# Moving a ninth MLP unit into the attention, and the first weight conversions into its first steps

## The chip, the cores and the metric

The kernel runs on one core of one Trainium2 chip. The metric is device time in microseconds of one execution, the median over several runs. TensorE ran at its upper clock level (2.4 GHz; mean granted clock 0.998) in the profiled execution.

## The reference

Attention with a soft cap over 4 batches, 12 heads, 448 tokens and head dimension 64, then a three-way maximum MLP over 1792 tokens of width 768, all float32.

```
scores = cap * tanh(scale * q @ k.T / cap)          # scale = 1 / sqrt(64)
attn   = exp(scores - max) ; attn = attn / (sum(attn) + 1e-9)
x      = (attn @ v)  with heads joined               # 1792 x 768
h      = max(max(x @ w1, x @ w2), x @ w3)            # 1792 x 768
out    = h @ w_out                                   # 1792 x 768
```

## The kernel before

**Attention.** A step t (0 to 11) handles one batch and a group of four heads; batch t // 3, group t % 3. Keys are cut into seven tiles j of 64. For each tile TensorE makes the scores (`scores`, L120: eight float32 matmul instructions on 64x64 quadrants) into one of two PSUM buffers `qk` in turn; ScalarE takes tanh out of PSUM (`tanh`, L129) and exp in SBUF (`expo`, L132); TensorE multiplies the exponentials with v (`values`, L135) into the PSUM tile `av`; VectorE adds the exponentials up (`add`, L143). At the start of the next step TensorE sums over the keys with a matrix of ones (`sums`, L147) into the PSUM tile `sm`, in two halves for the steps in BY_PE, whose seventh exponential TensorE adds instead of VectorE. VectorE makes the reciprocals with two transposes (`recip`, L157), multiplies (`normalize`, L166), and splits the result into a high and a low float32r part in `xx` (`split_x`, L170). The maximum is not subtracted: with a small cap the exponentials can't overflow, and a branch takes the general form otherwise.

**Order.** All orders are written out by hand. Function `step` (L268) lists the instructions of all engines in one sequence; each engine takes its own from it in order, and waits where an operand or buffer isn't ready. `scores(t+1, 0..2)` and `tanh(t+1, 0)` already stand at the end of step t, and `scores(t+1, 2)`, the last of them, needs the buffer that `tanh(t+1, 0)` reads.

**MLP units.** A unit (n, b) multiplies one weight tile n (128 outputs; n = 3f + w, matrix w of output tile f, n from 18 on for w_out) with the tokens of one block b: `products` (L227), 18 float32r matmuls, three for each of six input chunks. Block 0 has 256 tokens, blocks 1 to 3 have 512. Block 0 needs batch 0 (steps 0 to 2), block 1 steps 0 to 5, block 2 steps 0 to 8, block 3 all. `empty` (L238) copies the result with ScalarE for w = 0, and takes the maximum into it with VectorE for w = 1, 2. A table FILL puts eight units into the middle of steps 4 to 11, ahead of `scores(t, 5)`; they use half of `sm`. The unit (2,2) is done right behind the attention (FILLED), then units (0,3) and (1,3), whose chunks 4 and 5 come last because they need step 11. All other units follow in order of n and b (`mlp`, L379).

**Weights.** A weight tile arrives as 64-bit floats (768 KB), and six instructions (`conv`, L200, steps 0 to 5) make the float32r high and low parts. Tables CONV, SCALED and LOADS say in which attention steps these instructions and the DMAs stand; in step 0 the first tile's conversions stand between the adds. Tiles use two raw buffers `wd`, two work buffers `cw` and three result buffers `wh`, `wl`.

**Start and end.** `first` holds q of step 0 and the cap in one array of 897 columns; it, k, v and the first weight tile are loaded on ScalarE's DMA queue, later ones on SP's. The very last bank, (23, 3), is copied in two halves of 256 tokens, one by VectorE and one by ScalarE, each with its own store.

Of the kernel before, what the change touches and what calls it, by code (L numbers as in the profile page):

```python
# [29 lines left out]
CAP_LO = 1e-6  # L30
WARM = 7

FILL = {4 + i: (i % 3, i // 3) for i in range(8)}
FILLED = [(2, 2)]
BY_PE = (0, 1, 2, 3, 11)
CONV = {0: [(0, 4), (0, 5)], 1: [(1, 0), (1, 1)], 2: [(1, 2), (1, 3)], 3: [(1, 4), (1, 5), (2, 0)],
        4: [(2, 1), (2, 2)], 5: [(2, 3), (2, 4), (2, 5)], 9: [(3, 1)], 10: [(3, 2), (3, 3)]}
SCALED = {9: 3}
LOADS = {0: 1, 1: 2, 6: 3, 11: 4}


@with_exitstack
def attn_max_mlp_kernel(ctx: ExitStack, tc: tile.TileContext, first, q, k, v, wts, out):
# [113 lines left out]
    def recip(t, eps):  # L157
        x, r = x_t[t % 2], r_t[t % 2]
        nc.vector.transpose(out=x, in_=sm[:, :, 0:S])
        nc.vector.tensor_scalar_add(r, flat(x).rearrange("p (a b) -> p a b", b=32)[:, :, 0], eps)  # L160
        nc.vector.reciprocal(r, r)
        nc.vector.transpose(  # L162
            out=flat(x).rearrange("p (a b) -> p a b", b=32), in_=r.unsqueeze(2).to_broadcast([128, 2 * QB, 32])
        )
# [73 lines left out]
    def empty(n, b, ps):  # L238
        f, w = divmod(n, 3)
        at = slice(*BLOCKS[b])  # L240
        ps = ps[:, 0:at.stop - at.start]
        if n < 3 * KC:
            m = m_t[f][:, at]
            if w == 0:
                nc.scalar.copy(out=m, in_=ps)
            else:
                tt(nc.vector, m, m, ps, ALU.max)
            return
        dst = out[n - 3 * KC][:, at]
        o = o_t[outs[0] % len(o_t)][:, 0:at.stop - at.start]  # L250
        outs[0] += 1
        if (n, b) == (NU - 1, NB - 1):
            one, two = slice(0, 256), slice(256, 512)
            nc.vector.tensor_copy(out=o[:, one], in_=ps[:, one])
            nc.sync.dma_start(out=dst[:, one], in_=o[:, one])
            nc.scalar.copy(out=o[:, two], in_=ps[:, two])
            nc.scalar.dma_start(out=dst[:, two], in_=o[:, two])
        else:
            nc.scalar.copy(out=o, in_=ps)
            nc.sync.dma_start(out=dst, in_=o)  # L260
# [7 lines left out]
    def step(t, eps):  # L268
        last = t - 1
        if 0 < t < NG - 1:  # L270
            load_qk(t + 1)
        if t:
            sums(last, last in BY_PE)
            recip(last, eps)
        if t == NG:
            for j in range(4, NJ):
                values(last, j)
            normalize(last)
            split_x(last)
            return  # L280
        fill = FILL.get(t)
        tanh(t, 1)
        expo(t, 0)
        scores(t, 3)
        if t:
            values(last, 4)
            values(last, 5)
        tanh(t, 2)
        expo(t, 1)
        add(t, 1)  # L290
        scores(t, 4)
        if t:
            values(last, 6)
            normalize(last)
        tanh(t, 3)
        expo(t, 2)
        add(t, 2)
        if t:
            split_x(last)
        if 0 < t < NG - 1:  # L300
            load_v(t + 1)
        if t in LOADS:
            conv_load(LOADS[t])
        if fill:
            products(*fill, sm[:, 0, :], range(KC))
        tanh(t, 4)
        expo(t, 3)
        if fill:
            expo(t, 4)
            empty(*fill, sm[:, 0, :])  # L310
        if t in SCALED:
            conv(SCALED[t], 0, True)
        add(t, 3)
        if t == 0:
            conv(0, 0)
            conv(0, 1)
        scores(t, 5)
        if not fill:
            tanh(t, 5)
            expo(t, 4)  # L320
            scores(t, 6)
            values(t, 0)
        else:
            values(t, 0)
            tanh(t, 5)
            scores(t, 6)
        add(t, 4)
        if t == 0:
            conv(0, 2)
        values(t, 1)  # L330
        if t + 1 < NG:
            scores(t + 1, 0)
        values(t, 2)
        if fill:
            expo(t, 5)
            tanh(t, 6)
        else:
            tanh(t, 6)
            expo(t, 5)
        add(t, 5)  # L340
        if t == 0:
            conv(0, 3)
        if t + 1 < NG:
            scores(t + 1, 1)
        expo(t, 6)
        if t not in BY_PE:
            add(t, 6)
        for n, i in CONV.get(t, []):
            conv(n, i)
        values(t, 3)  # L350
        if t + 1 < NG:
            tanh(t + 1, 0)
            scores(t + 1, 2)

    def general_attention():
        for t in range(NG):
# [22 lines left out]
    def mlp(done, convs):  # L379
        g = 0  # L380

        def bank():
            nonlocal g
            g += 1
            return banks[(g - 1) % 8]

        def whole(n, b):
            ps = bank()
            products(n, b, ps, range(KC))
            empty(n, b, ps)  # L390
            done.add((n, b))

        fast = bool(done)
        if fast:
            for n, b in FILLED:
                whole(n, b)
            held = []
            for n in range(2):
                held.append(bank())
                products(n, NB - 1, held[n], range(KC - 2))  # L400
            for n in range(2):
                products(n, NB - 1, held[n], range(KC - 2, KC))
                empty(n, NB - 1, held[n])
                done.add((n, NB - 1))
                if n == 0:
                    for i in (4, 5):
                        conv(3, i, True)
        for n in range(NU):
            if 3 <= n and n + 2 < NU:
                conv_load(n + 2)  # L410
            for b in range(NB):
                if (n, b) not in done:
                    whole(n, b)
                if n >= 3 and n + 2 < NU:
                    for i in convs[b]:
                        conv(n + 2, i, True)
                elif n == 2 and b == NB - 1:
                    for i in range(6):
                        conv(4, i, True)
                elif not fast and n == 0 and b == NB - 1:  # L420
                    for i in (4, 5):
                        conv(3, i, True)
                if n == 3 * KC - 1:
                    for f in range(KC):
                        split_h(b, f)
# [2 lines left out]

    with tc.manual_schedule():
        nc.sync.dma_start(out=k_t[0][:, 0:2].rearrange("p a b c -> p (a b c)"), in_=k[0, :, 0:256])  # L430
        nc.scalar.dma_start(out=q_0[:, 0:2 * S + 1], in_=first)
        nc.scalar.dma_start(out=k_t[0][:, 2:].rearrange("p a b c -> p (a b c)"), in_=k[0, :, 256:])
        load_v(0, nc.scalar)
        conv_load(0, nc.scalar)
        nc.vector.memset(wz.bitcast(F32), 0.0)
        for _ in range(WARM):
            nc.tensor.matmul(sm[:, 0, 0:S], wz[:, 0:128], wz, start=True, stop=True)
        nc.gpsimd.memset(ones, 1.0)
        nc.gpsimd.memset(eps_g, 1e-9)
        nc.scalar.activation(out=acap, in_=cap_t, func=AF.Abs)  # L440
        nc.vector.tensor_scalar(out=fl, in0=acap, scalar1=CAP_HI, scalar2=None, op0=ALU.is_le)
        nc.vector.scalar_tensor_tensor(
            out=fl_i, in0=acap, scalar=CAP_LO, in1=fl, op0=ALU.is_ge, op1=ALU.mult
        )
        nc.vector.reciprocal(sc_t, acap)
        nc.vector.tensor_scalar_mul(sc_t, sc_t, 1.0 / float(D) ** 0.5)
        nc.scalar.activation(out=eps_f, in_=acap, func=AF.Exp, scale=-1.0)
        nc.vector.tensor_scalar_mul(eps_f, eps_f, 1e-9)
        scores(0, 0)
        scores(0, 1)  # L450
        tanh(0, 0)
        scores(0, 2)
        flag = nc.values_load(fl_i[0:1, 0:1], min_val=0, max_val=1)
        with tc.If(flag > 0) as br:
            load_qk(1)
            load_v(1)
            for t in range(NG + 1):
                step(t, eps_f)
            mlp({*FILL.values()}, convs)
        outs[0] = 0  # L460
        with br.Else():
            general_attention()
            conv_load(1)
            for n in range(3):
                for i in range(6):
                    conv(n, i)
                conv_load(n + 2)
            for i in range(4):
                conv(3, i)
            mlp(set(), convs)  # L470
# [49 lines left out]
```

## Time and profile before

| what | value |
|---|---|
| median of 3 runs | 509.86 us (509.38 to 510.35) |
| profiled execution, its own time | 509.67 us |
| span of its trace | 507.9 us |
| busy VectorE, ScalarE | 259.8 us (51%), 229.3 us (45%) |
| attention (steps 0 to 11 with the last normalization) | up to about 183.5 us |

The span is the time from the first to the last instruction; the time of an execution is 1.8 us longer. Engine names in the rows: PE is TensorE, PEld its weight loads, DVE is VectorE, ACT is ScalarE, SPq and ACTq are DMA issues of these queues. An instruction's line is that of the helper that records it, so L102 is every VectorE operation on two tensors, and the tile names tell which one it is.

### The profile page before, as it was taken

The numbers are of one execution on the slowest core, as the hardware profiler recorded it, in microseconds if no ns is written. First come the engines' busy times: TensorE is split into PE (matmuls) and PEld (weight loads), VectorE is DVE, ScalarE is ACT, GpSimd is POOL, SyncE is SP. The second block draws the span as 40 slices with busy tenths as digits, with TensorE's granted clock in tenths as the row PEclk, the third lists the DMA queues.
The fourth block names the chain that finished last, engine by engine and source line by source line (L and its number), as shares of the span: only waits on it lengthen the run. The fifth ranks groups of instructions, "written<-read, shape, count | busy, mean of one in ns | idle before, by whom it ended". The sixth has DMA issues, their size and how long they took to land.

```text
span 507.9 us, 7474 instructions
## 1 busy us (share of the span) xinstructions
PE 494.1 (97%) x3215; PEld 350.7 (69%) x3215; DVE 259.8 (51%) x332; ACT 229.3 (45%) x285; POOL 0.4 (0%) x6
## 2 busy tenths in 40 slices
PE   6899999999999999999999999999999999999996
PEld 2333344444455568888888888888888888888884
DVE  1889999987778963334323413332341577212000
ACT  6999999979888711410121121021122355221210
POOL 0000000000000000000000000000000000000000
PEclk9999999999999999999999999999999999999999
DMA  7343333413232100301301111120121101333111
GB/s 280 135 172 111 110 110 110 167 42 110 74 111 98 63 1 0 125 12 52 124 1 62 63 62 63 41 85 0 63 72 54 63 1 52 136 114 136 69 56 68
DMA packets 12423, 41.44 MB, mean 82 GB/s; under 512 B 1376, under 2 KB 2528, under 8 KB 12384
## 3 DMA queue, kind: packets, MB, share of 16 engines
q1 hardware_dynamic: 11664, 38.74, 22.0%
q10 hardware_dynamic: 720, 2.16, 1.1%
q8 instruction: 27, 0.44, 0.3%
q14 instruction: 12, 0.10, 0.1%
HBM read 35.39 MB, written 5.51 MB: 81 GB/s over the span
## 4 chain that ended last, share of the span: by engine, by line
PE 88%; ACT 6%; DVE 3%; issue 1%; DMA 1%; ACTq 0%; DVEq 0%
PE qk L232 9%; PE qk L233 9%; PE qk L234 9%; PE qk L124 9%; PE av L138 8%; PE sm L232 8%; PE sm L234 8%; PE sm L233 8%; PE av L234 6%; PE av L232 6%; PE av L233 6%; ACT e_all L130 3%; ACT e_all L133 3%; PE sm L152 3%; DVE s_t L102 1%
## 5 line engine op out<-in xcount | busy, mean ns | idle before, releaser
L232 PE MATMUL qk<-xx,wh 128*128 128x512 f32 (+1 forms) x264 | 89.6, 339 | 0.0
L233 PE MATMUL qk<-xx,wh 128*128 128x512 f32 (+1 forms) x264 | 89.6, 339 | 0.0
L234 PE MATMUL qk<-xx,wl 128*128 128x512 f32 (+1 forms) x264 | 89.3, 338 | 0.0
L130 ACT ACTIVATE e_all<-qk,sc_t 128x896 f32<-128x896 f32 x84 | 83.3, 1006 | 10.9 <-PE qk L124 10.4
L133 ACT ACTIVATE e_all<-e_all,acap 128x896 f32<-128x896 f32 x84 | 86.5, 1046 | 0.5
L124 PE MATMUL qk<-q,k_t 64*64 64x448 f32 x672 | 78.7, 543 | 7.0 <-ACT e_all L130 6.2
L138 PE MATMUL av<-e_all,v_t 64*64 64x448 f32 x672 | 74.9, 536 | 0.0
L221 ACT CAST wh<-cw 128x768 fp32r<-128x768 f32 x21 | 17.5, 835 | 116.2 <-DVE cw L217 116.2
L232 PE MATMUL sm<-xx,wh 128*128 128x512 f32 (+1 forms) x180 | 69.0, 383 | 0.0
L234 PE MATMUL sm<-xx,wl 128*128 128x512 f32 (+1 forms) x180 | 68.2, 379 | 0.0
L233 PE MATMUL sm<-xx,wh 128*128 128x512 f32 (+1 forms) x180 | 68.1, 378 | 0.0
L102 DVE TENSOR_TENSOR s_t<-s_t,e_all 128x896 f32<-128x896 f32 x55 | 59.8, 1088 | 10.3 <-ACT e_all L133 8.3
L124 PEld LDWEIGHTS qk<-q,k_t 64*64 64x64 f32 x672 | 23.2, 132 | 47.1 <-ACT e_all L130 21.5
L232 PEld LDWEIGHTS qk<-xx,wh 128*128 128x128 f32 x264 | 50.1, 190 | 6.3 <-issue 0.7
L234 PEld LDWEIGHTS qk<-xx,wl 128*128 128x128 f32 x264 | 50.0, 189 | 5.6
L233 PEld LDWEIGHTS qk<-xx,wh 128*128 128x128 f32 x264 | 50.1, 190 | 5.4
L138 PEld LDWEIGHTS av<-e_all,v_t 64*64 64x64 f32 x672 | 25.5, 133 | 37.6 <-issue 36.1
L232 PE MATMUL av<-xx,wh 128*128 128x512 f32 x132 | 51.3, 389 | 0.0
L233 PE MATMUL av<-xx,wh 128*128 128x512 f32 x132 | 51.3, 389 | 0.0
L234 PE MATMUL av<-xx,wl 128*128 128x512 f32 x132 | 51.3, 389 | 0.0
L102 DVE TENSOR_TENSOR wl<-cw,wh 128x768 fp32r<-128x768 f32 x24 | 23.0, 956 | 42.9 <-ACT wh L221 35.4
L232 PEld LDWEIGHTS sm<-xx,wh 128*128 128x128 f32 x180 | 33.8, 188 | 11.7 <-DVE x_t L162 4.9
(66 smaller groups left out, 414.8 us busy)
## 6 DMA issues: line engine op xcount, KB each, us to landing
wd<-in_wts_dram SPq DMA_DIRECT2D x23, 768.0 KB, 4.2
k_t<-in_k_dram SPq DMA_DIRECT2D x11, 448.0 KB, 3.4
q<-in_q_dram SPq DMA_DIRECT2D x11, 448.0 KB, 4.5
v_t<-in_v_dram SPq DMA_DIRECT2D x11, 448.0 KB, 3.3
out_dram<-q SPq DMA_DIRECT2D x6, 256.0 KB, 2.0
out_dram<-s_t SPq DMA_DIRECT2D x6, 256.0 KB, 2.0
out_dram<-x_t SPq DMA_DIRECT2D x5, 256.0 KB, 2.0
wd<-in_wts_dram ACTq DMA_DIRECT2D x1, 768.0 KB, 6.9
```

The costliest lines, as they stand in the source:

```text
L102: eng.tensor_tensor(out=out, in0=in0, in1=in1, op=op)
L124: nc.tensor.matmul(ps[rows(s), R, 0:S], k_t[t % 2][rows(R), j, s, :], q_t[t % 2][rows(R), s, :], start=True, stop=True, skip_group_check=True,
L130: nc.scalar.activation(out=e_of(t, j), in_=slot(t, j)[:, :, 0:S], func=AF.Tanh, scale=sc_t)
L133: nc.scalar.activation(out=e_of(t, j), in_=e_of(t, j), func=AF.Exp, scale=acap)
L138: nc.tensor.matmul(av[rows(R), s, 0:S], v_t[t % 2][rows(s), j, R, :], e_of(t, j)[rows(s), R, :], start=(j == 0), stop=(j == NJ - 1), skip_ ...
L152: nc.tensor.matmul(sm[rows(R), s, 0:S], ones[rows(s), :], part[rows(s), R, :], start=(i == 0), stop=(i == len(parts) - 1), skip_group_chec ...
L221: nc.scalar.copy(out=h, in_=d)
L232: nc.tensor.matmul(ps, w_h, a_h, start=(kc == 0), stop=False)
L233: nc.tensor.matmul(ps, w_h, a_l, start=False, stop=False)
L234: nc.tensor.matmul(ps, w_l, a_h, start=False, stop=(kc == KC - 1))
```

## The change

Unit (2,2) moves into the attention. Units (0,0), (0,1) and (0,2) now stand at the end of steps 3, 6 and 9 (table LATE), behind `scores(t+1, 2)`, and are emptied in the next step ahead of its sums; the other six stand in the middle of steps 4, 5, 7, 8, 10 and 11. The sums in steps 4, 7 and 10 move behind `scores(t, 3)` and the emptying. Weight tiles 0 and 1 are both converted in step 0, tile 2 in steps 1 to 3 (it was steps 3 to 5), and the first two instructions of tile 3 move from step 9 to step 8. The loads of weight tile 0 and 1 are both issued at the start, tile 0 ahead of v. `first` gets 960 columns in DRAM, of which 897 are loaded. The last weight tile takes its blocks in the order 1, 2, 3, 0, so that the last bank has 256 tokens, copied in halves of 128.

```
-FILL = {4 + i: (i % 3, i // 3) for i in range(8)}
-FILLED = [(2, 2)]
+LATE = {3: (0, 0), 6: (0, 1), 9: (0, 2)}
+FILL = {4: (1, 0), 5: (2, 0), 7: (1, 1), 8: (2, 1), 10: (1, 2), 11: (2, 2)}
-CONV = {0: [(0, 4), (0, 5)], 1: [(1, 0), (1, 1)], 2: [(1, 2), (1, 3)], 3: [(1, 4), (1, 5), (2, 0)],
-        4: [(2, 1), (2, 2)], 5: [(2, 3), (2, 4), (2, 5)], 9: [(3, 1)], 10: [(3, 2), (3, 3)]}
-SCALED = {9: 3}
-LOADS = {0: 1, 1: 2, 6: 3, 11: 4}
+CONV = {1: [(2, 0), (2, 1)], 2: [(2, 2), (2, 3)], 3: [(2, 4), (2, 5)], 8: [(3, 1)], 10: [(3, 2), (3, 3)]}
+SCALED = {8: 3}
+LOADS = {1: 2, 6: 3, 11: 4}
+FIRST = {0: [(0, 0), (0, 1), (0, 2), (0, 3)], 1: [(0, 4), (0, 5)], 2: [(1, 0)], 3: [(1, 1)], 4: [(1, 2)],
+         5: [(1, 3), (1, 4), (1, 5)]}
...
-        if (n, b) == (NU - 1, NB - 1):
-            one, two = slice(0, 256), slice(256, 512)
+        if (n, b) == (NU - 1, 0):
+            one, two = slice(0, 128), slice(128, 256)
...
+        late, fill = LATE.get(last), FILL.get(t)
...
+        if t and not late:
+            normalizing()                     # sums(last), recip(last)
...
+        if t == 0:
+            convs(FIRST[0])                   # FIRST[j] stands behind add(0, j) for j = 1 to 5
         tanh(t, 1)
         expo(t, 0)
         scores(t, 3)
+        if late:
+            tanh(t, 2)
+            empty(*late, sm[:, 0, :])
+            normalizing()
         if t:
             values(last, 4)
             values(last, 5)
-        tanh(t, 2)
+        if not late:
+            tanh(t, 2)
         expo(t, 1)
         add(t, 1)
...
         if t + 1 < NG:
             tanh(t + 1, 0)
             scores(t + 1, 2)
+        if t in LATE:
+            products(*LATE[t], sm[:, 0, :], range(KC))
...
-            for n, b in FILLED:
-                whole(n, b)
...
-            for b in range(NB):
+            for b in range(NB) if n < NU - 1 else (1, 2, 3, 0):
...
-        nc.scalar.dma_start(out=q_0[:, 0:2 * S + 1], in_=first)
+        nc.scalar.dma_start(out=q_0[:, 0:2 * S + 1], in_=first[:, 0:2 * S + 1])
         nc.scalar.dma_start(out=k_t[0][:, 2:].rearrange("p a b c -> p (a b c)"), in_=k[0, :, 256:])
+        conv_load(0, nc.scalar)
         load_v(0, nc.scalar)
-        conv_load(0, nc.scalar)
+        conv_load(1, nc.scalar)
...
-            [qq[0, 0].reshape(128, 2 * S), _np.broadcast_to(_np.asarray(inputs["cap"]).reshape(1, 1), (128, 1))], axis=1
+            [qq[0, 0].reshape(128, 2 * S), _np.broadcast_to(_np.asarray(inputs["cap"]).reshape(1, 1), (128, 64))], axis=1
```

## Rows read from the trace of the kernel before

**Rows 1.** The page, busy time, share of the span and instructions by engine.
```profile
PE 494.1 (97%) x3215; PEld 350.7 (69%) x3215; DVE 259.8 (51%) x332; ACT 229.3 (45%) x285; POOL 0.4 (0%) x6
```

**Rows 2.** Windows: length, busy us (instructions) by engine, clock, DMA share, GB/s.
```profile
46.16:59.19 13.03, 12.25 (x129) 4.71 (x129) 12.42 (x15) 12.90 (x15) 0.00 (x0) 1.00 0.34 108
150.37:166.15 15.78, 15.78 (x143) 7.70 (x139) 12.31 (x14) 13.72 (x17) 0.00 (x0) 1.00 0.22 80
```

**Rows 3.** Timeline, TensorE, steps 3 to 7: start, us, engine, line, operation, [idle before].
```profile
59.19 0.98 PE L124 MATMUL qk<-q,k_t 64*64 64x448 f32 x8 [0.78 <-ACT e_all L130]
...
81.54 0.98 PE L124 MATMUL qk<-q,k_t 64*64 64x448 f32 x8
...
87.60 0.97 PE L124 MATMUL qk<-q,k_t 64*64 64x448 f32 x8
...
101.43 0.98 PE L124 MATMUL qk<-q,k_t 64*64 64x448 f32 x8
102.95 0.98 PE L152 MATMUL sm<-s_t,ones 64*64 64x448 f32 x8 [0.54 <-DVE s_t L102]
...
107.62 0.50 PE L232 MATMUL sm<-xx,wh 128*128 128x512 f32 x1
...
111.94 0.98 PE L124 MATMUL qk<-q,k_t 64*64 64x448 f32 x8
```

**Rows 4.** Timeline, TensorE, step 9: two group starts, seven groups apart.
```profile
144.32 0.93 PE L138 MATMUL av<-e_all,v_t 64*64 64x448 f32 x8
...
149.58 0.97 PE L124 MATMUL qk<-q,k_t 64*64 64x448 f32 x8
```

**Rows 5.** Timeline, TensorE, the first matmuls of the last two units.
```profile
494.64 0.39 PE L232 MATMUL sm<-xx,wh 128*128 128x512 f32 x1
...
498.72 0.39 PE L232 MATMUL av<-xx,wh 128*128 128x512 f32 x1
```

**Rows 6.** Timeline, from the attention's end: unit (2,2) begins; the last subtraction.
```profile
183.52 0.50 PE L232 MATMUL qk<-xx,wh 128*128 128x512 f32 x1
...
186.20 1.09 DVE L102 TENSOR_TENSOR xx<-x_t,xx 128x896 fp32r<-128x896 f32 x1
```

**Rows 7.** Timeline, ScalarE, steps 3 to 7.
```profile
58.13 1.90 ACT L130 ACTIVATE e_all<-qk,sc_t 128x896 f32<-128x896 f32 x2
...
82.59 1.01 ACT L130 ACTIVATE e_all<-qk,sc_t 128x896 f32<-128x896 f32 x1 [0.63 <-PE qk L124]
...
93.80 1.98 ACT L133 ACTIVATE e_all<-e_all,acap 128x896 f32<-128x896 f32 x2
...
112.05 0.59 ACT L245 COPY m<-sm 128x512 f32<-128x512 f32 x1 [2.14 <-PE sm L234]
```

**Rows 8.** Timeline, VectorE, steps 5 and 6.
```profile
75.60 1.12 DVE L159 STREAM_TRANSPOSE x_t<-sm 128x896 f32<-128x896 f32 x1 [0.18 <-PE sm L152]
...
83.06 0.41 DVE L102 TENSOR_TENSOR m<-m,sm 128x256 f32<-128x256 f32 x1
...
98.22 4.67 DVE L102 TENSOR_TENSOR s_t<-s_t,e_all 128x896 f32<-128x896 f32 x4
```

**Rows 9.** Windows, step 0 from the first add to the first transpose.
```profile
11.00:22.64 11.64, 9.03 (x93) 3.37 (x96) 9.59 (x11) 11.64 (x14) 0.00 (x0) 1.00 0.53 196
```

**Rows 10.** The same window, instructions on `cw` alone: VectorE, ScalarE busy.
```profile
11.00:22.64 11.64, 4.55 (x6) 0.00 (x0) 1.00 0.53 196
```

**Rows 11.** Timeline, ScalarE's DMA queue: issue of the first weight tile.
```profile
2.13 0.45 ACTq L198 DMA_DIRECT2D wd<-in_wts_dram  x1
```

**Rows 12.** DMA issues on ScalarE's queue: count, KB each, median us to landing.
```profile
wd<-in_wts_dram ACTq DMA_DIRECT2D x1, 768.0 KB, 6.9
...
out_dram<-x_t ACTq DMA_DIRECT2D x1, 128.0 KB, 2.4
```

**Rows 13.** Timeline, the last two copies out of PSUM.
```profile
503.05 0.42 DVE L254 COPY x_t<-av 128x256 f32<-128x256 f32 x1 [30.62 <-PE av L234]
...
503.51 0.37 ACT L256 COPY x_t<-av 128x256 f32<-128x256 f32 x1 [3.96 <-DVE x_t L254]
```

More of the change, by code (lines that the diff above doesn't have):

```diff
@@ L271, in step, with convs, normalizing @@
             load_qk(t + 1)
-        if t:
+        late, fill = LATE.get(last), FILL.get(t)
+        def convs(pieces):
+            for n, i in pieces:
+                conv(n, i)
+        def normalizing():
             sums(last, last in BY_PE)
             recip(last, eps)
+        if t and not late:
+            normalizing()
         if t == NG:
@@ L280, in step @@
             return
-        fill = FILL.get(t)
+        if t == 0:
+            convs(FIRST[0])
         tanh(t, 1)
@@ L287, in step @@
             values(last, 5)
-        tanh(t, 2)
+        if not late:
+            tanh(t, 2)
         expo(t, 1)
         add(t, 1)
+        if t == 0:
+            convs(FIRST[1])
         scores(t, 4)
@@ L297, in step @@
         add(t, 2)
-        if t:
+        if t == 0:
+            convs(FIRST[2])
+        else:
             split_x(last)
@@ L314, in step @@
         if t == 0:
-            conv(0, 0)
-            conv(0, 1)
+            convs(FIRST[3])
         scores(t, 5)
@@ L328, in step @@
         if t == 0:
-            conv(0, 2)
+            convs(FIRST[4])
         values(t, 1)
@@ L341, in step @@
         if t == 0:
-            conv(0, 3)
+            convs(FIRST[5])
         if t + 1 < NG:
@@ L347, in step @@
             add(t, 6)
-        for n, i in CONV.get(t, []):
-            conv(n, i)
+        convs(CONV.get(t, []))
         values(t, 3)
@@ L458, in attn_max_mlp_kernel @@
                 step(t, eps_f)
-            mlp({*FILL.values()}, convs)
+            mlp({*FILL.values(), *LATE.values()}, convs)
         outs[0] = 0
@@ L462, in attn_max_mlp_kernel @@
             general_attention()
-            conv_load(1)
             for n in range(3):
```

## The prediction

> **What bounds the kernel now.** I read the page's busy line first. TensorE is busy 494.1 of 507.9 us [rows 1], so the change can win only from the 13.8 us in which TensorE stands still, or lose by adding to them. The windows view, cut at one step of the attention, shows two kinds of step. A step without an MLP unit (46.16 to 59.19) lasts 13.03 us; ScalarE is busy 12.90 of them with 14 activations, 0.92 us each, while TensorE has 12.25. A step with a 512-token unit (150.37 to 166.15) lasts 15.78 us, TensorE fills all of it and ScalarE has only 13.72 [rows 2]. So steps 0 to 3 are set by ScalarE and steps 4 to 11 by TensorE. The timeline of TensorE then gives the idle places: 0.78 us before the last scores of an unfilled step, where tanh of the next step's first tile still holds the score buffer, and one wait for VectorE before the sums at 102.95 [rows 3]. In the three-matrix phase TensorE has no wait. The rest of its idle time is the start, where ScalarE sets the pace from its first activation on, and about 5 us behind the last unit (498.72 + 4.08 against 507.9 [rows 1, 5]).
>
> **Units of cost.** One group of eight small matmuls (scores, values or sums) takes 0.751 us: seven groups in 5.26 [rows 4]. A step has 15 groups (16 where TensorE adds the last exponent), 11.27 us. A step with a 256-token unit lasts 13.83 (87.60 to 101.43), so that unit costs 2.56; with a 512-token unit 15.78, so that unit costs 4.51 [rows 2, 3]. Of this 4.32 are its matmuls (107.62 to 111.94), the rest the change between the two matmul shapes. In the three-matrix phase a 512 unit takes 4.08 (494.64 to 498.72) [rows 5].
>
> **The ninth unit.** The attention keeps its three 256 units and gets a sixth 512 unit: +4.51. The phase behind it loses (2,2): -4.08. TensorE's own work thus grows by 0.43. What (2,2) covered was the last normalization. Behind it stand 24 matmuls on head groups 0 to 3, 24 x 4.08/18 = 5.44 us, which need nothing of step 11. In the trace the last subtraction of the split, begun at 186.20, ended 3.8 us after (2,2) began at 183.52 [rows 6], so these still cover it, and I cost that at nothing. Were they too short, the price would be what is missing, at most 1 us.
>
> **Steps 6 and 9 become unfilled.** Here is the main term. The plan now fills steps 4, 5, 7, 8, 10, 11 in their middle; the units of 3, 6 and 9 stand behind scores(t+1,2), the step's last scores. TensorE takes its queue in order, so a unit placed there cannot fill a hole ahead of those scores. Take Y as the start of scores(5,5), right behind step 5's unit: 81.54 before [rows 3]. TensorE alone needs from Y to scores(7,2) 6.06 (81.54 to 87.60) + 11.27 = 17.33 us. ScalarE starts tanh(5,5) 1.05 after Y, at 82.59, and from then on runs without a hole to exp(6,3) at 93.80 [rows 7]. In an unfilled step exp(6,3) is followed by tanh, exp, tanh, exp, exp and tanh(7,0), which is six starts later: 93.80 + 6 x 0.92 = 99.32. The buffer is free 1.06 after that start (tanh pair at 58.13, scores at 59.19 [rows 3, 7]), so scores(7,2) start at 100.38, Y + 18.84. TensorE therefore idles 18.84 - 17.33 = 1.51 us in step 6, and by the same chain in step 9: +3.02. Below this lies 0 (ScalarE carries a lead over), above it 2 a step (a wait of tanh(t,4) on top, as steps 1 to 3 have).
>
> **Step 3 wins nothing.** Its 0.78 us hole stands ahead of the late unit as well, so (0,0) merely moves from the middle of step 4 to the end of step 3.
>
> **The late steps 4, 7, 10.** The sums now wait for the ScalarE copy of the late unit, because both use one PSUM tile. Queued behind them are values, scores(t,4) and the next unit. The copy starts 0.11 after scores(t,3) do (111.94 to 112.05) and takes 0.59 [rows 3, 7], and scores(t,3) take 0.80, so they hide it. Uncovered it would cost 0.6 in steps 7 and 10, 0.4 in step 4. ScalarE itself waits about 2 us for a 512 unit, which it can afford. The VectorE chain behind the sums starts later, however. Call P the start of the second half of sums(3). The first transpose starts 1.0 after it (0.93 to 0.98 until the group has drained, and the handover), the max of unit (1,0) 7.46 later (75.60 to 83.06), which takes 0.41; then come four dependent adds, 4.67, and the sums 0.06 after their end (98.22 + 4.67 against 102.95): P + 13.6 [rows 3, 8]. TensorE would be there at P + 0.75 + 4 x 0.75 + 2.51 + 6.06 + 0.79 = P + 13.1 (its group, four more, the unit, eight groups, the last scores). So sums(4) wait 0.5 us (bounds 0 and 1). In steps 7 and 10 the longer unit gives TensorE 1.95 us more, which covers it.
>
> **Conversions.** Steps 4 and 5 lose theirs. That removes the wait at 102.95: 102.95 - 101.43 - 0.75 = 0.77, so -0.77 [rows 3, 8]. In step 0 the first four conversions go ahead of the first add, at 11.00, and six more come in. From 11.00 to 22.64 VectorE was busy 9.59 us, idle 2.05 [rows 9]; the six conversions of one tile, all in that stretch, took 4.55 [rows 10]. The stretch loses the first four of them, about two thirds (3.0), and gets a whole tile: +1.5, inside the 2.05. New waits: conv(0,0) waits for its weights with add(0,1) and everything else of VectorE behind it; conv(1,0) the same, with add(0,3) behind it. The first tile landed 6.9 us after an issue at 2.13 [rows 11, 12]; issued earlier and ahead of v, it lands at 7.5 to 9.0, and the four conversions end at 10.6 to 12.1 against the add's 11.0. From there up to 0.8 us of lateness is swallowed by the hole of step 1. I take 0, with bounds -0.1 and +0.7. ScalarE's fifth DMA issue costs 0.45 us [rows 11] while it still waits for its first operand, so nothing; SP loses one.
>
> **First load.** The row pitch of `first` grows from 3588 to 3840 bytes; bytes and number of rows that are moved stay. The start hangs on this load. No row tells what a pitch costs. The two landings of [rows 12] differ by 4.5 us for 640 KB; at that rate these 448 KB stream for 3.2 us, and a sixth of that either way is 0.5. I take 0, between -0.5 and +0.5, as the nearest row is the load itself, which moves the same packets. The Trainium skill (DMA: Bandwidth & Descriptors, section How a descriptor splits into AXI transactions) says that a descriptor that does not start on a 256-byte boundary fetches unused bytes below its start; by it some 4 of 113 beats go, an estimate of 0.05 us, and the sum would be 512.5 instead of 512.6. No row here shows that effect.
>
> **The end.** The last bank has 256 tokens, so each half is 128 wide. Now VectorE copies 256 in 0.42 and ScalarE, behind it, 256 in 0.37 against 0.59 for 512 [rows 7, 13]: a halving saves about 0.14 and 0.11. The last 128 KB landed 2.4 us after their issue [rows 12]; no row has 64 KB, I take the same, between that and 0.35 less. Together -0.25 (bounds 0 and -0.6). The 512 bank ahead of it is copied beside the last unit's matmuls.
>
> **Sum.** +4.51 - 4.08 + 3.02 + 0.5 - 0.77 - 0.25 = +2.9. On the profiled execution's own 509.67 this is 512.6; the median of the runs, 509.86, is 0.2 higher, which I leave in the range.
>
> **Rivals.** *Not slower: ScalarE carries a lead into steps 6 and 9.* In filled steps it idles while the unit runs (0.6 us at 256 tokens, about 2 at 512 [rows 7]). Were that time used for work of the next step, the 1.51 in each would vanish: 512.6 - 3.0 = 509.6, and without the VectorE wait 509.1, no change. It decides from a lead of 1.5 us in both steps. Against it: tanh(t,5) needs scores(t,5), which stand behind the unit in TensorE's queue, and the row at 82.59 shows ScalarE starting 1.05 after them. For faster, -0.5 from the first load must come on top: 508.6. *The start turns late.* Were the second weight tile to land at 16 us, add(0,3) and the sums behind it would push ScalarE by 0.5 to 0.7: 513.3. Against it: it is requested before step 0, where it was requested in that step's body. *The copy is not hidden in the late steps*: +1.6, 514.2; for it speaks that the margin is 0.1 us. *The conversions' wait at 102.95 stays* (the change does less than it says): 513.4; against it, the five conversions of steps 4 and 5, which pushed VectorE's chain back, are gone from there.
>
> **Chances.** Forecast 0.68; late start or copy 0.12; wait stays 0.05; lead carried over 0.11; that with a faster first load 0.04. A difference under 0.2% (1.0 us) cannot be told from none. Slower 0.85, within 0.11, faster 0.04. The range leaves the lead case and the far ends out: 511.0 to 513.9.
>
> **What would show it.** In the profile after: TensorE waits of 1.3 to 1.6 us on tanh before the last scores of steps 6 and 9, as in steps 1 to 3; a wait of about 0.5 on VectorE's add before sums(4); none before the sums of steps 7 and 10; the wait at 102.95 gone; three-matrix phase shorter by 4.1; about 4.7 us behind the last matmul. Wrong it is if steps 6 and 9 are TensorE-bound, or the start moves by over 0.5 us.

## The result, and the profile after

The changed kernel takes 513.44 us (median of 6 runs, 512.63 to 513.96); the kernel before took 510.08 in the same runs (6, 509.38 to 510.35). The ratio is 1.0068, 95% interval 1.0055 to 1.0081: slower by 3.4 us, where the forecast said 2.9 (512.6, range 511.0 to 513.9). The span of the profiled execution grew from 507.9 to 511.5.

The busy line of the page after, against [rows 1]:

```profile
span 511.5 us, 7492 instructions
PE 496.0 (97%) x3215; PEld 350.5 (69%) x3215; DVE 259.6 (51%) x332; ACT 228.8 (45%) x285; POOL 0.4 (0%) x6
```

TensorE stands still for 511.5 - 496.0 = 15.5 us (13.8 before) and is busy 1.9 us more: 0.71 of that in its first sixteen small matmuls (see the start below), 0.41 in the ninth unit, most of the rest in the drain behind the new stops. The work of the other engines is the same. So the loss is a matter of order, and the windows view shows where. Cut from the last scores of one step to those of the next, against [rows 2] (length, busy us of TensorE, its weight loads, VectorE, ScalarE, GpSimd, clock, DMA share, GB/s), steps 6 and 9:

```profile
91.01:103.80 12.79, 11.74 (x125) 4.39 (x121) 11.01 (x13) 12.79 (x15) 0.00 (x0) 1.00 0.49 176
139.87:152.64 12.77, 11.72 (x124) 4.37 (x120) 11.23 (x14) 12.77 (x15) 0.00 (x0) 1.00 0.35 114
```

In both ScalarE is busy for the whole window, and TensorE is not: these two steps changed their bound. TensorE's timeline has the stops one by one, against [rows 3] (a wait stands in brackets at the end of its row):

```profile
59.49 0.98 PE L125 MATMUL qk<-q,k_t 64*64 64x448 f32 x8 [0.77 <-ACT e_all L131]
...
62.75 0.98 PE L125 MATMUL qk<-q,k_t 64*64 64x448 f32 x8
...
76.58 0.97 PE L125 MATMUL qk<-q,k_t 64*64 64x448 f32 x8
77.91 0.98 PE L153 MATMUL sm<-s_t,ones 64*64 64x448 f32 x8 [0.36 <-DVE s_t L103]
...
84.93 0.98 PE L125 MATMUL qk<-q,k_t 64*64 64x448 f32 x8
...
96.33 2.04 PE L125 MATMUL qk<-q,k_t 64*64 64x448 f32 x16
...
103.80 0.98 PE L125 MATMUL qk<-q,k_t 64*64 64x448 f32 x8 [0.92 <-ACT e_all L131]
...
109.04 0.98 PE L125 MATMUL qk<-q,k_t 64*64 64x448 f32 x8
109.84 0.93 PE L153 MATMUL sm<-s_t,ones 64*64 64x448 f32 x8
...
133.80 0.98 PE L125 MATMUL qk<-q,k_t 64*64 64x448 f32 x8
...
152.64 0.98 PE L125 MATMUL qk<-q,k_t 64*64 64x448 f32 x8 [0.92 <-ACT e_all L131]
```

Step 6: scores(5,5) at 84.93, scores(7,2) at 103.80, 18.87 us apart, of which TensorE needs 17.33. One part of the stop is in brackets. The other hides in the row at 96.33, two groups of scores that take 2.04 us where two in a row take 1.68: scores(6,6) waited 0.36 for tanh(6,4), which reads the buffer that they need. Step 9 is the same, 133.80 to 152.64. ScalarE's rows give the chain that sets step 6, against [rows 7]:

```profile
86.01 1.01 ACT L131 ACTIVATE e_all<-qk,sc_t 128x896 f32<-128x896 f32 x1 [1.17 <-PE qk L125]
...
102.72 1.92 ACT L131 ACTIVATE e_all<-qk,sc_t 128x896 f32<-128x896 f32 x2
```

It starts tanh(5,5) 1.08 after TensorE starts scores(5,5), has no wait from there to tanh(7,0) at 102.72, and scores(7,2) start 1.08 after that.

Back on TensorE, step 3's stop of 0.77 is still there, ahead of its late unit. The wait at 102.95 of [rows 3] is gone: sums(6) at 109.84 follow their predecessor without a gap. Instead sums(4) at 77.91 stand 0.54 later than a group would let them.

That wait is VectorE's. Its timeline in step 4, against [rows 8]:

```profile
65.40 1.12 DVE L160 STREAM_TRANSPOSE x_t<-sm 128x896 f32<-128x896 f32 x1 [3.98 <-PE sm L153]
...
72.85 0.42 DVE L103 TENSOR_TENSOR m<-m,sm 128x256 f32<-128x256 f32 x1
73.19 4.67 DVE L103 TENSOR_TENSOR s_t<-s_t,e_all 128x896 f32<-128x896 f32 x4
```

The chain cannot begin before 65.40, because the sums stand behind the late unit, and its last add ends at 73.19 + 4.67 = 77.86, just ahead of the sums at 77.91.

**The balance by the two traces.** Each line is a distance between rows. The last matmul before, and after:

```profile
502.57 0.39 PE L234 MATMUL av<-xx,wl 128*128 128x512 f32 x1
```

```profile
506.14 0.28 PE L235 MATMUL sm<-xx,wl 128*128 128x256 f32 x1
```

| term | forecast | in the traces |
|---|---|---|
| steps 6 and 9 unfilled | +3.02 | 18.87 and 18.84 less 17.33 each: +3.05 |
| ninth unit, in and out | +0.43 | 103.80 to 109.04 less one group of 0.75: 4.49 - 4.08 = +0.41 |
| wait before sums(4) | +0.5 | 77.91 - 76.58 - 0.79 = +0.54 |
| wait before sums(6) | -0.77 | gone: -0.77 |
| start, up to scores(4,2) | 0 | 59.49 against 59.19: +0.30 |
| behind the last matmul | -0.25 | 5.08 against 4.94: +0.14 |
| sum | +2.9 | +3.67; the spans differ by 3.6 |

The first four terms can be read in one piece. From the start of ScalarE's first tanh (6.23 before, 6.55 after) to the end of the last matmul it is 496.73 us before and 499.87 after: +3.14, where the forecast's terms for this stretch add up to +3.18. What is left of the change, 0.3 at the start and 0.1 at the end, lies outside it.

### The profile page after: what moved, and what is told of

The parts are those of the page before. It is cut to its first block, busy times and chain, and to the rows that moved or that the text cites. A ratio compares the mean times of both kernels' runs of the same rounds, so it can differ in the third digit from the quotient of the medians.

```text
span 511.5 us, 7492 instructions
## 1 busy us (share of the span) xinstructions
PE 496.0 (97%) x3215; PEld 350.5 (69%) x3215; DVE 259.6 (51%) x332; ACT 228.8 (45%) x285; POOL 0.4 (0%) x6
## 4 chain that ended last, share of the span: by engine, by line
PE 80%; ACT 11%; DVE 5%; issue 3%; DMA 1%; ACTq 0%; DVEq 0%
PE qk L233 12%; PE qk L234 12%; PE qk L235 12%; PE sm L233 8%; PE sm L235 8%; PE sm L234 8%; ACT e_all L131 6%; PE qk L125 5%; PE av L139 4%; ACT e_all L134 4%; PE av L235 3%; PE av L234 3%; PE av L233 3%; PE sm L153 2%; DVE s_t L103 2%
## 5 line engine op out<-in xcount | busy, mean ns | idle before, releaser
L233 PE MATMUL qk<-xx,wh 128*128 128x512 f32 x264 | 103.1, 391 | 0.0
L234 PE MATMUL qk<-xx,wh 128*128 128x512 f32 x264 | 103.0, 390 | 0.0
L235 PE MATMUL qk<-xx,wl 128*128 128x512 f32 x264 | 102.7, 389 | 0.0
L233 PE MATMUL sm<-xx,wh 128*128 128x512 f32 (+1 forms) x186 | 70.9, 381 | 0.0
L234 PE MATMUL sm<-xx,wh 128*128 128x512 f32 (+1 forms) x186 | 69.9, 376 | 0.0
L235 PE MATMUL sm<-xx,wl 128*128 128x512 f32 (+1 forms) x186 | 69.9, 376 | 0.0
L233 PEld LDWEIGHTS sm<-xx,wh 128*128 128x128 f32 x186 | 35.0, 188 | 12.5 <-issue 4.2
L103 DVE TENSOR_TENSOR e_all<-e_all,qk 128x512 f32<-128x512 f32 x20 | 13.8, 688 | 52.8 <-PE qk L235 52.8
L235 PEld LDWEIGHTS sm<-xx,wl 128*128 128x128 f32 x186 | 35.0, 188 | 6.4
L234 PEld LDWEIGHTS sm<-xx,wh 128*128 128x128 f32 x186 | 35.0, 188 | 6.2
```

Of the source, the lines that this page charges most:

```text
L103: eng.tensor_tensor(out=out, in0=in0, in1=in1, op=op)
L233: nc.tensor.matmul(ps, w_h, a_h, start=(kc == 0), stop=False)
L234: nc.tensor.matmul(ps, w_h, a_l, start=False, stop=False)
L235: nc.tensor.matmul(ps, w_l, a_h, start=False, stop=(kc == KC - 1))
```

## The experiments

Line numbers move by a few between kernels. Every time stands against runs of the kernel before on the same chip, 510.03 to 510.06 us.

**Old unit plan.** Only the conversions, their loads and the pitch are new.

```
-LATE = {3: (0, 0), 6: (0, 1), 9: (0, 2)}
-FILL = {4: (1, 0), 5: (2, 0), 7: (1, 1), 8: (2, 1), 10: (1, 2), 11: (2, 2)}
+LATE = {}
+FILL = {4 + i: (i % 3, i // 3) for i in range(8)}
+FILLED = [(2, 2)]
...
```

The lines left out do (2,2) behind the attention and make (23, 3) the last bank again.

> The changed kernel with the unit plan and the end of the kernel before; only the conversions, their loads and the row pitch of the first load are new. Theory A (steps 6 and 9 are unfilled, 3.0 us; the ninth unit 0.4; VectorE's wait before sums(4) 0.5): all of these go, the wait of 0.8 before sums(6) is gone too, and the start is some 0.3 late as in the profile after, so 509.5 to 509.8, 0.3 to 0.6 below the kernel before. Theory B (the six added conversions in step 0 and the earlier loads cost the time): it stays near 513.

508.91 us, ratio 0.9979 (0.9967 to 0.9991): faster than the kernel before, and 4.5 us faster than the changed one. Theory B falls: the six added conversions in step 0 cost nothing. In its trace the sums follow the last scores of step 6 without the old wait (against 102.95 in [rows 3]):

```profile
101.78 0.98 PE L126 MATMUL qk<-q,k_t 64*64 64x448 f32 x8
102.58 0.93 PE L154 MATMUL sm<-s_t,ones 64*64 64x448 f32 x8
```

The phase behind the attention begins at 183.09, against 183.52 in [rows 6], although scores(4,2) came 0.36 later (59.55): 0.79 us won, the 0.77 of the forecast. The median fell by 1.1, with an interval of about 0.6 either way, and lies below the 509.5 to 509.8 that was expected. From the first tanh to the last matmul it is 495.93 us, 0.80 less than the kernel before.

**Steps 6 and 9 filled.** Two units are done twice, one in the middle of each step, so the result stays and the work grows by one unit of 256 and one of 512.

```
-FILL = {4: (1, 0), 5: (2, 0), 7: (1, 1), 8: (2, 1), 10: (1, 2), 11: (2, 2)}
+FILL = {4: (1, 0), 5: (2, 0), 6: (2, 0), 7: (1, 1), 8: (2, 1), 9: (2, 1), 10: (1, 2), 11: (2, 2)}
```

> The changed kernel with two units done a second time, (2,0) in the middle of step 6 and (2,1) in the middle of step 9, so that all steps from 4 on are filled there; the result is the same, the work is more by 2.56 and 4.51 us. Theory A: each fills a hole of 1.5 us and costs only what is above it, 1.05 and 3.0: 517.5. Theory C (TensorE bound already in steps 6 and 9, the time lost in the late handover): the full 7.1 more, 520.5.

517.47 us, ratio 1.0149 (1.0126 to 1.0172). The extra work of 7.07 us costs 4.0. The last scores of steps 6 and 9, at 104.91 and 156.74, have no wait any more (those of steps 5 and 8 stand ahead of them):

```profile
91.09 0.97 PE L125 MATMUL qk<-q,k_t 64*64 64x448 f32 x8
...
104.91 0.97 PE L125 MATMUL qk<-q,k_t 64*64 64x448 f32 x8
...
140.95 0.97 PE L125 MATMUL qk<-q,k_t 64*64 64x448 f32 x8
...
156.74 0.97 PE L125 MATMUL qk<-q,k_t 64*64 64x448 f32 x8
```

The steps last 13.82 and 15.79 us, 1.03 and 3.02 more than the 12.79 and 12.77 of the changed kernel; each unit cost 1.5 less than its price in a full step. This is the main term, measured by itself. Theory C, which put the loss into the handover, asked for 7.1.

**Late unit ahead of the last scores.** Same nine units, one place earlier in TensorE's queue.

```
         values(t, 3)
+        if t in LATE:
+            products(*LATE[t], sm[:, 0, :], range(KC))
         if t + 1 < NG:
             tanh(t + 1, 0)
             scores(t + 1, 2)
-        if t in LATE:
-            products(*LATE[t], sm[:, 0, :], range(KC))
...
-            tanh(t, 2)
             empty(*late, sm[:, 0, :])
+            tanh(t, 2)
```

> The changed kernel, but the late units of steps 3, 6 and 9 stand ahead of scores(t+1,2) instead of behind, and ScalarE empties them ahead of tanh(t,2). Theory A: the unit then fills the hole in front of those scores, 0.8 us in step 3 and about 1.0 in steps 6 and 9, and a hole of 0.4 before scores(6,6) and scores(9,6) stays: 510.4 to 510.8. Theory C (what costs is the late units' handover, sums behind a copy and VectorE's later chain, not the unfilled steps): no gain, 513 to 514.

509.96 us, ratio 1.0002 (0.9993 to 1.0011): level with the kernel before, 3.5 us below the changed one, where 2.6 to 3.0 were expected (by the two traces 3.3 between the first tanh and the last matmul). Theory C, by which nothing is won, falls. Steps 6 and 7 in TensorE's timeline:

```profile
95.14 2.04 PE L125 MATMUL qk<-q,k_t 64*64 64x448 f32 x16
...
100.77 0.93 PE L139 MATMUL av<-e_all,v_t 64*64 64x448 f32 x8
...
105.94 1.73 PE L125 MATMUL qk<-q,k_t 64*64 64x448 f32 x16
107.50 0.93 PE L153 MATMUL sm<-s_t,ones 64*64 64x448 f32 x8
```

The unit runs from 101.6 on, right behind values(6,3), and scores(7,2) follow it at 105.94 without a wait; the 0.36 before scores(6,6) stays (again 2.04). The copy does hide: sums(6) start 1.56 after scores(7,2), two groups.

**VectorE's wait before sums(4).** In step 4 the split of step 3's result moves behind the adds.

```
-        else:
+        elif t != 4:
             split_x(last)
...
             add(t, 6)
+        if t == 4:
+            split_x(last)
```

> The changed kernel, but in step 4 VectorE splits the result of step 3 (1.65 us) behind the adds instead of ahead of them. The prediction's term: VectorE's chain sets sums(4), the wait of 0.4 to 0.5 us before them goes, and the time is 0.4 less than the changed kernel, 513.0; the later split delays the next transposes by less than TensorE's lead. If the wait comes from elsewhere, it stays, 513.4.

513.33 us, ratio 1.0061 (1.0041 to 1.0082), where 513.0 was expected: the time alone cannot tell 0.4 us. The trace can:

```profile
60.38 0.98 PE L125 MATMUL qk<-q,k_t 64*64 64x448 f32 x8 [0.77 <-ACT e_all L131]
...
77.47 0.97 PE L125 MATMUL qk<-q,k_t 64*64 64x448 f32 x8
78.26 0.93 PE L153 MATMUL sm<-s_t,ones 64*64 64x448 f32 x8
...
104.09 0.98 PE L125 MATMUL qk<-q,k_t 64*64 64x448 f32 x8 [0.92 <-ACT e_all L131]
```

The wait is gone, and from scores(4,2) to scores(7,2) it is 43.71 us instead of 44.31. The profiled execution took 513.79 all the same, as its start was 0.9 us later (60.38 against 59.49); see the start below.

**The end undone.**

```
-        if (n, b) == (NU - 1, 0):
-            one, two = slice(0, 128), slice(128, 256)
+        if (n, b) == (NU - 1, NB - 1):
+            one, two = slice(0, 256), slice(256, 512)
...
-            for b in range(NB) if n < NU - 1 else (1, 2, 3, 0):
+            for b in range(NB):
```

> The changed kernel with the last tile's blocks in the old order 0 to 3, the last bank 512 wide and copied in halves of 256. The prediction's term: 0.25 us slower than the changed kernel, 513.7. The profile after (5.08 us from the last matmul's end to the span's end against 4.94 before): no difference, 513.3 to 513.4.

513.52 us, ratio 1.0064 (1.0048 to 1.0080): no difference from the changed kernel, as its trace had said. The copies and stores did get shorter. The changed kernel's last two copies, against [rows 13]:

```profile
506.51 0.29 DVE L255 COPY x_t<-sm 128x128 f32<-128x128 f32 x1 [30.59 <-PE sm L235]
...
506.84 0.27 ACT L257 COPY x_t<-sm 128x128 f32<-128x128 f32 x1 [1.90 <-DVE x_t L255]
```

That is 0.13 and 0.10 us less. What they save is lost behind them. The last store, here and with the old end:

```profile
507.13 0.35 ACTq L258 DMA_DIRECT2D out_dram<-x_t  x1
```

```profile
507.70 0.35 ACTq L258 DMA_DIRECT2D out_dram<-x_t  x1
```

The spans end at 511.5 and 511.6: 4.4 and 3.9 us later. Over all thirteen profiles this stretch is 3.9 to 4.1 us in the six with 128 KB stores at the end, and 4.4 to 5.0 in the seven with 64 KB. SP waits in it for the stores to land and for TensorE's queue. The waits of the SP queue (who waits for whom: us in total, times, longest) of the changed kernel, of the one with the old order of loads (below; the same end), and of the one with the old end:

```profile
SPq L533 <- PEq L533: 2.0, 2, 1.6
...
SPq L533 <- DMA out_dram<-x_t: 1.2, 2, 1.1
```

```profile
SPq L534 <- DMA out_dram<-x_t: 2.6, 2, 1.4
...
SPq L534 <- PEq L534: 0.7, 2, 0.4
```

```profile
SPq L533 <- DMA out_dram<-x_t: 1.7, 2, 1.1
SPq L533 <- PEq L533: 1.1, 2, 0.7
```

The waits add up to 3.2, 3.3 and 2.8. With 64 KB they take two forms: four profiles look like the first, where ScalarE's store lands in 2.0 to 2.3 us and TensorE's queue is late, three like the second, where that store takes 3.3 to 3.4 (128 KB: 2.4 to 2.5). The sum is longer in both. Why smaller stores end later was not tried, nor were the size of the stores and the width of the last unit taken apart: both changed together.

**The start.** Three runs take the load apart, two the warming matmuls, and one repeats the kernel before. First the old pitch:

```
-        nc.scalar.dma_start(out=q_0[:, 0:2 * S + 1], in_=first[:, 0:2 * S + 1])
+        nc.scalar.dma_start(out=q_0[:, 0:2 * S + 1], in_=first)
...
-            [qq[0, 0].reshape(128, 2 * S), _np.broadcast_to(_np.asarray(inputs["cap"]).reshape(1, 1), (128, 64))], axis=1
+            [qq[0, 0].reshape(128, 2 * S), _np.broadcast_to(_np.asarray(inputs["cap"]).reshape(1, 1), (128, 1))], axis=1
```

`first` has 897 columns in DRAM again.

> The changed kernel with the first load from rows of 897 columns again (pitch 3588 bytes). If the pitch brought the first load in 0.4 us earlier (4.0 against 4.4 us to landing), it lands at 5.1 again; if the scores behind it then run at their full rate, as in the kernel before, the time is 0.3 us shorter than the changed kernel, 513.1; if pitch does nothing, landing stays at 4.0 us and the time at 513.4.

513.32 us, ratio 1.0063 (1.0050 to 1.0076); landing 4.0 us with this pitch too. Pitch does nothing that shows. The rule of the Trainium skill cited in the prediction (DMA: Bandwidth & Descriptors, How a descriptor splits into AXI transactions) is neither borne out nor refuted: its estimate was 0.05 us, below what these runs resolve.

The old order of loads:

```
-        conv_load(0, nc.scalar)
         load_v(0, nc.scalar)
-        conv_load(1, nc.scalar)
+        conv_load(0, nc.scalar)
...
             load_v(1)
+            conv_load(1)
```

> The changed kernel with the loads of the kernel before: v ahead of the first weight tile, the second weight tile on SP's queue after q, k and v of step 1. The prediction's bound for a late weight tile: the first tile lands at 9.0 and the second at about 16, add(0,3) and sums(0) wait behind conv(1,0), and the time is 0.5 to 0.7 more than the changed kernel, 514.0. If the start has that much room, 513.4. Landing of the first load: 4.4 us again if the order of the loads behind it set it, 4.0 if not.

513.10 us, ratio 1.0055 (1.0035 to 1.0075): not slower. The weights come later, and VectorE waits for both:

```profile
8.75 0.59 DVE L208 TENSOR_SCALAR cw<-wd 128x768 f32<-128x768 f32 x1 [3.08 <-DMA wd<-in_wts_dram]
...
15.74 0.57 DVE L208 TENSOR_SCALAR cw<-wd 128x768 f32<-128x768 f32 x1 [0.36 <-DMA wd<-in_wts_dram]
...
22.15 0.96 DVE L103 TENSOR_TENSOR wl<-cw,wh 128x768 fp32r<-128x768 f32 x1
23.05 1.12 DVE L160 STREAM_TRANSPOSE x_t<-sm 128x896 f32<-128x896 f32 x1
```

They cost nothing all the same. From the first tanh to the first transpose it is 16.42 us here (6.63 to 23.05), 16.40 in the changed kernel and 16.41 in the kernel before. So the bound of +0.7 for a late weight tile was too wide; the room in step 0 takes it.

What moves the start is seen in the first sixteen small matmuls. In the changed kernel the first load lands at 4.7 us, earlier than in the old profile, yet ScalarE begins later (its first row before was at 6.23):

```profile
4.77 2.45 PE L125 MATMUL qk<-q,k_t 64*64 64x448 f32 x16 [0.41 <-DMA q<-in_first_dram]
```

```profile
6.55 1.90 ACT L131 ACTIVATE e_all<-qk,sc_t 128x896 f32<-128x896 f32 x2 [1.36 <-PE qk L125]
```

Sixteen took 1.74 in the old profile and take 2.45 here. The clock column reads 1.00 in both, but it counts time for which a trace holds no clock record as 1.00. The first clock record kept with a trace is the rise to 2.4 GHz. It stands at 4.58 us in the old profile, before the sixteen start, and at 6.28 in the changed kernel, in their midst. Latest it stands in the run with the later split, at 9.52, and there the weight loads show TensorE's pace ahead of it:

```profile
5.80 0.25 PEld L125 LDWEIGHTS qk<-q,k_t 64*64 64x64 f32 x4 [0.50 <-issue]
6.55 0.25 PEld L125 LDWEIGHTS qk<-q,k_t 64*64 64x64 f32 x4 [0.50 <-issue]
```

Four matmuls take 0.75 us, where eight take 0.751 later [rows 4]: half the pace, so the lower of the two clock levels, 1.2 GHz. In the eleven profiles in which one row holds the sixteen, they took 1.74 us plus half of what lay between their start and the rise, within 0.05 us. Ahead of them TensorE had done the warming matmuls from 1.38 us on and, with seven of these, stood still for 0.4 to 0.8.

Nine warming matmuls instead of seven, on the kernel with the old unit plan:

> The kernel of e1_old_units with nine warming matmuls instead of seven, so that TensorE works on until about 5.2 us instead of 4.4. In the profiles with the new loads the first load lands at 4.7 to 4.8 us, but the first scores then take about twice as long a group (0.75 us per four matmuls and their weights instead of 0.38) and the first tanh starts at 6.3 to 6.7. If TensorE's pace there hangs on what it did just before, the first tanh starts at 6.1 to 6.2 and the time falls by 0.3 us or more, 508.6. If it does not, the scores only start later, the first tanh at 6.9 and 0.3 us more, 509.2.

509.28 us, ratio 0.9982 (0.9971 to 0.9993). The sixteen took 1.73 (rise at 4.85), ScalarE began at 6.03, and yet the median is not below 508.91. The same on the kernel before, and the kernel before again:

> The kernel before with nine warming matmuls. If TensorE's pace at the first scores hangs on what it did just before, the first sixteen run at full rate and the first tanh starts at 6.0 to 6.2; the median then falls by 0.2 to 0.5, 509.6. If not, nothing or 0.2 more.

> The kernel before, unchanged, for a second profile of its start. In the nine profiles taken since, the first load landed 3.9 to 4.2 us after its issue with either pitch and either order of the loads behind it, and the first sixteen small matmuls mostly ran at half their rate. If the old start (landing 4.4, full rate, scores(4,2) at 59.19) belongs to the kernel before, it shows again; if it was one draw among those that any of these kernels can have, landing is 4.0 to 4.2 and the first tanh somewhere between 6.2 and 6.9.

With nine warming matmuls the kernel before took 509.99, ratio 1.0000 (0.9991 to 1.0009); its sixteen took 2.27 (rise at 6.18) and ScalarE began at 6.64. Repeated unchanged it landed its first load in 4.1 us, its sixteen took 1.98 (rise at 5.46), and ScalarE began at 6.21.

Over the thirteen profiles the rise lies between 4.58 and 9.52 us and ScalarE's first tanh between 6.03 and 6.84. With seven warming matmuls the two profiles of the kernel before have their first tanh at 6.21 and 6.23, and all eight with the new loads have it later, at 6.34 to 6.84. With nine it is the other way round, 6.64 against 6.03 and 6.17. So whether the 0.3 us at the start in the balance above belong to the change stays open, and so does what sets the moment of the rise; neither the old pitch alone (rise at 5.85) nor the old order of loads alone (6.76) brings the old start back. Warming longer does not show in the medians.

**The best with nine units.** The late unit ahead, the later split and nine warming matmuls together:

> The kernel of e2_unit_ahead with the later split of e6_split_later and nine warming matmuls. Theory A: 0.4 from VectorE's wait before sums(4), 0 to 0.4 from the start, against 509.96: 509.2 to 509.6, which leaves nine units 0.3 to 0.7 above the eight of e1_old_units (a unit costs 0.43 more in the attention, and the holes of 0.4 before scores(6,6) and scores(9,6) stay, against the 0.8 of step 3 that it fills).

509.62 us, ratio 0.9993 (0.9983 to 1.0003), just above the 509.2 to 509.6 that was expected. It wins back 3.8 us of the changed kernel and stays level with the kernel before. The old unit plan with the new conversions has the lowest medians, 508.91 and 509.28. The traces put that distance outside the attention and the MLP: from the first tanh to the last matmul it is 495.93 us here and 495.93 with the old unit plan, so the ninth unit, placed like this, neither costs nor gains anything there. What differs is the end, 5.0 us from the last store's issue against 4.0, and the start.

## Why the prediction was right

**Main term.** "TensorE therefore idles 18.84 - 17.33 = 1.51 us in step 6, and by the same chain in step 9" held to 0.03 us, and in the run with both steps filled the price of the units fell by just that. The chain held link by link: 1.08, 17.79 and 1.08 us in the rows above, where the forecast had 1.05, 17.78 and 1.06. The rival in which ScalarE carries a lead into these steps is refuted by the same rows: tanh(5,5) waits 1.17 us for its scores, and from there ScalarE is busy from end to end. One sign was not quite as written. The wait does not stand in one piece before the last scores: 0.92 is in brackets there, and 0.36 stands earlier, before scores(6,6). A wait of that kind, on tanh(t,4), was named for the upper bound of 2 a step, on top of the 1.51; here it is part of it.

**The ninth unit.** It was put at +0.43 and measured +0.41. That the last normalization stays covered held too: the last subtraction ends 3.8 us after the first unit behind the attention begins (194.87 and 191.09), and no wait of TensorE on `xx` appears. The phase behind the attention is 4.1 us shorter, as forecast.

**Step 3.** "Its 0.78 us hole stands ahead of the late unit as well" held: 0.77 in the changed kernel, none when the unit is moved ahead.

**Late steps.** The copy was hidden, so the rival that charged 1.6 us for it is out. The wait on VectorE's chain was put at 0.5 and was 0.54.

**Conversions.** The wait before sums(6) went, worth its 0.77, and step 0 had room. The bound of +0.7 on a late weight tile was not needed even with the old loads.

**What was off.** "Together -0.25" for the end: it measured +0.14 by the traces (5.08 us behind the last matmul, where the sign said 4.7) and nothing by the times. The copies fell by 0.23 as worked out. The term is off because the landing was the only thing priced behind them ("I take the same"): in the changed kernel's profile the last store landed in 2.0 us, even sooner than the 2.4 assumed, but SP's waits at the end add up to 3.2 instead of 2.9, and from the issue to the end of the span it takes 4.4 to 5.0 us with 64 KB against 3.9 to 4.1. The start was put at nothing and was 0.3 later by the traces; its cause is the moment of the clock's rise, which no term of the sum holds, and whether the change moved it is open. The rival of a late start had named a late second weight tile, which the 16.40 us from the first tanh to the first transpose rule out. These two small misses have the same sign. Without the -0.25 the sum would have been 3.2, against 3.4 between the medians. The rest of the distance from 512.6 to 513.44 is mostly the base: 509.67, one execution, where the kernel before had a median of 510.08 in the same runs. In the text on the first load, the estimate of 0.05 us for 4 of 113 beats does not come from its own streaming time of 3.2 us, which would give 0.11; the sum of 512.5 stays the same with either.

## What to carry to other kernels

Filler work on an in-order queue has a price that depends on its place: in a step that another engine bounds it is partly free, in a step that is full it costs all of itself. Moving a filler from the middle of a step to behind the step's last dependent instruction takes it out of the hole it filled; count the holes that open in the step it left, not only the ones it may close. Where a late handover is needed, put the filler ahead of the instruction that waits, and test two edits made together apart: here the conversions were worth 1.1 us by the medians (0.8 by the traces) and the unit plan cost 4.5 (3.9 between the first tanh and the last matmul).

## What the runs showed of the hardware that was not expected

The first sixteen small matmuls took between 1.73 and 2.68 us in the eleven profiles that show them in a row of their own, with the clock column at 1.00. The rise to 2.4 GHz came between 4.58 and 9.52 us in the thirteen profiles, though the warming matmuls began at 1.38 in all of them, and up to it TensorE ran at half its later pace; the mean clock of a span, 0.998 for the kernel before, leaves that stretch out. And a smaller last store need not end a kernel sooner: from its issue to the end of the span it took 4.4 to 5.0 us with 64 KB, 3.9 to 4.1 with 128 KB; what of it is the store's size and what the last unit's width was not separated.
